# Fourier mixing and an MLP on one core: VectorE's sums of w2, a pinned opening, one load queue, filler matmuls

## The chip, the core and the metric

The kernel runs on one core of a Trainium2 chip. The core has TensorE (PE, matmuls and transposes, which write to PSUM), VectorE (DVE), ScalarE (ACT), GpSimd (POOL) and SyncE (SP, here only a queue that issues DMA transfers). Each engine works through its own queue in order and waits on semaphores for the others. The metric is the device time of one execution in microseconds; lower is better.

## The reference

Input x is 2048 x 576. Its rows are normalized (layernorm without weights) to xn, and the output is a sum of three terms:

```python
a = einsum("bsd,ed->bse", xn, dft_hid_re)
b = einsum("bsd,ed->bse", xn, dft_hid_im)
y = einsum("ts,bse->bte", dft_seq_re, a) - einsum("ts,bse->bte", dft_seq_im, b)
h = maximum(einsum("bsd,df->bsf", xn, w1), 0)
return x + y + einsum("bsf,fd->bsd", h, w2)
```

w1 is 576 x 4608 and w2 is 4608 x 576. All inputs are float32.

## The kernel before

**Numbers.** A float32 operand is scaled by a power of two and split into two float16 halves, hi on ScalarE (L164) and lo = src * s - hi on VectorE (L165). A product then takes three float16 products (hi hi, hi lo, lo hi). The power of two comes from a maximum of absolute values: for w1 by VectorE (`magnitude`, L98), for w2 as a sum of absolute values by ScalarE (`sum_w2`, L374). For blocks 0 and 1 the maximum over partitions goes through TensorE (`power_pe`, L134 to L157: a small matmul, a reduction on VectorE, a second small matmul, three small VectorE steps); for later blocks GpSimd does it.

**Tiling.** x is 16 tiles of 128 rows, four of them a group of 512. The hidden width is nine blocks of 512, each in four slices of 128. For each block and group the first layer (`mlp1`) is 4 x 14 matmuls of 512 columns; `mlp1_out` applies the ReLU, splits, and forms the sums of a Strassen-Winograd scheme; the second layer (`mlp2`) is seven products of 12 matmuls of 288 columns, each followed by an accumulation into `acc` in SBUF on VectorE (L334). Products 0, 2, 4 and 6 use one PSUM bank pair and add up in it, 1 uses another, 3 and 5 a third; so product 2 can start only after the accumulation of product 0 has read the bank. The scheme needs four sums of quarters of w2 for each half block (`sums_w2`, L404 to L407): they are made by GpSimd for blocks 0 and 1 and by VectorE for later blocks. The DFT follows after the nine blocks.

**The opening.** x is loaded into `acc`, tile by tile, and w1 into a pool of two buffers (tag `raw`) which w2 shares. Each tile of x is normalized: `stats` (L175: two statistics, a merge, a square root on ScalarE and six small steps on VectorE), `normalize` (L219: xn on VectorE, its float16 half from x on ScalarE), `remainder` (L227: xn minus its half, on GpSimd but for tile 0) and `transposes` (L236: nine transposes on TensorE into a PSUM slot, then two copies to SBUF on ScalarE, L245 and L248). In block 0 the first layer runs tile by tile for tiles 0 to 3, and for tiles 4 to 7 in the first two slices (`tile_by`, groups of 14 matmuls of 128 columns), so that it can start on the first tile. `power_pe`, `transposes`, the first layer's sums for tiles 4 to 7 (`pq`) and `mlp2` take their PSUM from one pool of two slots (tag `ps2`).

**What sets the order.** The code is written through a scheduler, which places the instructions of each engine in an order of its own choice, by program order as a priority and by its estimate of when operands are ready. Nothing of the opening is pinned. `weave` (L208) interleaves the small steps of the statistics with other calls. x and most of w1 are issued from SyncE's queue; w1's first half block from ScalarE's (L446). The main loop (L605) runs over pairs of block and group: at each step it issues the first layer of this pair, the second layer of the previous pair, and pieces of the next block's preparation from a list (`todo`, `prepare_block`).

Of the kernel before, what the change touches and what calls it, by code (L numbers as in the profile page):

```python
# [41 lines left out]
def kernel(  # L42
# [43 lines left out]
    def load_w1(b, i, parts=1, eng=nc.sync):  # L86
        r = raws["w1", b, i] = raw.tile([P, 2 * KT, P], F32, tag="raw", name=f"raw_w1_{b}_{i}")
        n = 2 * KT // parts
        for k in range(0, 2 * KT, n):
            eng.dma_start(r[:, k : k + n], w1[b, i][:, k : k + n])  # L90
# [5 lines left out]
    def magnitude(dst, src):  # L96

        nc.vector.tensor_reduce(dst, src, AX.XY, ALU.max, apply_absolute_value=True)  # L98

    def power(s, p, m):  # L100
# [12 lines left out]
        )  # L113

# [19 lines left out]
    def power_pe(s, p, m):  # L134
# [4 lines left out]
        for c in range(n):  # L139
            nc.tensor.matmul(  # L140
                ps[:1, 0, c * P : (c + 1) * P], m[:, c : c + 1], ident.bitcast(BF16),
                start=True, stop=True,
            )
        top = small.tile([1, n], BF16, tag=f"top{n}", name="top")
        nc.vector.tensor_reduce(
            top, ps[:1, 0, : n * P].rearrange("p (n f) -> p n f", f=P), AX.X, ALU.max
        )
        nc.tensor.matmul(ps[:, 1, :n], ones, top, start=True, stop=True)
        half = small.tile([P, n], F32, tag=f"half{n}", name="half")
        nc.vector.tensor_scalar(half, ps[:, 1, :n], 2.0**-107, 2.0**6, ALU.max, ALU.mult)  # L150
        nc.vector.tensor_scalar(
            s.bitcast(I32), half.bitcast(I32), EXPONENT, EXPONENT,
            ALU.bitwise_and, ALU.bitwise_xor,
        )
        nc.vector.tensor_scalar(
            p.bitcast(I32), half.bitcast(I32), EXPONENT, None, ALU.bitwise_and
        )  # L157
# [4 lines left out]
    def split(hi, lo, src, s):  # L162

        nc.scalar.activation(hi, src, AF.Copy, scale=s)  # L164
        nc.vector.scalar_tensor_tensor(lo, src, s, hi, ALU.mult, ALU.subtract)  # L165
# [9 lines left out]
    def stats(ts):  # L175
# [3 lines left out]
        sts = [small.tile([P, 2, 6], F32, tag="st", name=f"st{t}", bufs=4) for t in ts]  # L179
        for t, st in zip(ts, sts):  # L180
            for j in range(2):
                nc.vector.bn_stats(st[:, j, :], acc[t][:, j * EH : (j + 1) * EH])
                yield
        for i, st in enumerate(sts):
            nc.vector.bn_aggr(mv[:, i], st.rearrange("p a b -> p (a b)"))
            yield
# [13 lines left out]
        nc.vector.tensor_scalar(u, u, -0.5 * SX, 1.5 * SX, ALU.mult, ALU.add)  # L200
        yield
        nc.vector.tensor_tensor(r, u, r0, ALU.mult)
        yield
        stt(sh, m, -1.0, r, ALU.mult, ALU.mult)
# [3 lines left out]
    def weave(steps, *others):  # L208

        others = list(others)  # L210
        for _ in steps:
            if others:
                others.pop(0)()
        for f in others:
            f()

    xns, xss = {}, {}

    def normalize(t, eng=nc.vector):  # L219
# [4 lines left out]
        eng.tensor_scalar(xn, acc[t], means[t], factors[t], ALU.subtract, ALU.mult)  # L224
        nc.scalar.activation(xs[:, :D], acc[t], AF.Identity, bias=shifts[t], scale=factors[t])

    def remainder(t, eng):  # L227
        xn, xs = xns[t], xss[t]
        eng.tensor_tensor(
            xs[:, D : D + REM], xn[:, KM * P :], xs[:, KM * P : D], ALU.subtract  # L230
        )
        eng.tensor_tensor(
            xs[:, D + REM :], xn[:, : KM * P], xs[:, : KM * P], ALU.subtract
        )

    def transposes(t):  # L236
        xs = xss[t]
        pt = ps2.tile([P, 2, 1024], F16, tag="ps2", name=f"pt{t}")
        for k in range(NKX):
            nc.tensor.transpose(  # L240
                pt[:, k // 8, (k % 8) * P : (k % 8 + 1) * P], xs[:, k * P : (k + 1) * P], ident
            )
        g, c = divmod(t, TG)
        dst = xT[g][:, :, c * P : (c + 1) * P]
        nc.scalar.activation(  # L245
            dst[:, :8, :], pt[:, 0, :].rearrange("p (k t) -> p k t", t=P), AF.Copy
        )
        nc.scalar.activation(dst[:, 8, :], pt[:, 1, :P], AF.Copy)  # L248
# [35 lines left out]
    def mlp1_group(b, g, i, cols, ps, wk=WK):  # L284
        for n, (kx, hl, k) in enumerate(wk):
            nc.tensor.matmul(  # L286
                ps[:, cols], w1s[b, i // 2][:, hl, i % 2 * KT + k], xT[g][:, kx, cols],
                start=(n == 0), stop=(n == len(WK) - 1),
            )
# [6 lines left out]
    def mlp1_out(b, g, i, pa, pb):  # L296
# [6 lines left out]
        nc.scalar.activation(r21, a21, AF.Relu)  # L303
        for q, src in ((slice(A11, A11 + 1), a11), (slice(A12, A22 + 1), pb)):
            hi, lo = (h[:, n, q].rearrange("p a b -> p (a b)") for n in range(2))
            nc.scalar.activation(hi, src, AF.Relu)  # L306
            stt(lo, src, 0.0, hi, ALU.max, ALU.subtract)  # L307
        stt(s3, a11, 0.0, r21, ALU.max, ALU.subtract)
        stt(s1, a22, 0.0, r21, ALU.max, ALU.add)
        stt(s2, a22, 0.0, s3, ALU.max, ALU.subtract)  # L310
        stt(s4, a12, 0.0, s2, ALU.max, ALU.subtract)  # L311
        hi, lo = (h[:, n, S1 : S4 + 1] for n in range(2))
        order["s"] = nc.scalar.activation(hi, st[:, 1:], AF.Copy).ins  # L313
        nc.vector.tensor_tensor(lo, st[:, 1:], hi, ALU.subtract)  # L314
# [3 lines left out]
    def mlp2(b, g, n):  # L318
# [5 lines left out]
        for c in range(2):  # L324
            for i in range(NQ):
                h, w = hs[b, g, i], w2s[b, i]
                for j, (x, y) in enumerate(((0, 0), (0, 1), (1, 0))):
                    nc.tensor.matmul(  # L328
# [3 lines left out]
                    )  # L332
        o = accs[g].rearrange("p (h c) (j e) -> p h j c e", h=2, j=2)[:, row, col]
        nc.vector.scalar_tensor_tensor(o, ps, us[b], o, ALU.mult, ALU.add)  # L334
# [6 lines left out]
    def max_w1(b, f):  # L341
# [7 lines left out]
        magnitude(mx["f", b][:, r : r + 1], raws["w1", b, i][:, r * KT : (r + 1) * KT])  # L349
        if r:  # L350
            m = mx["w1", b][:, i : i + 1] if b > 1 else mx["b", i]
            nc.vector.tensor_reduce(m, mx["f", b], AX.X, ALU.max)

    def power_w1(b, i):
# [3 lines left out]
        else:  # L358
            power_pe(s, p, mx["b", i])
# [8 lines left out]
    def sum_w2(b, i):  # L368
# [5 lines left out]
        nc.scalar.activation(  # L374
            junk, raws["w2", b, i], AF.Abs, scale=2.0**-10, accum_out=mx["w2", b][:, i : i + 1]
        )

    def power_w2(b):
# [3 lines left out]
        else:  # L382
            m = small.tile([P, NQ], BF16, tag="mb2", name=f"mb2_{b}")
            nc.vector.tensor_copy(m, mx["w2", b])
# [452 lines left out]
```

## Time and profile before

| | us |
|---|---|
| median of 3 runs (lowest to highest) | 1305.89 (1304.32 to 1306.62) |
| profiled execution | 1306.57 |
| its span | 1304.8 |
| TensorE busy in the span | 1274.5 |
| VectorE busy | 968.0 |
| ScalarE busy | 532.8 |
| GpSimd busy | 49.7 |

Times of the trace count from the span's start. A group of instructions is shown by line, engine, operation, output and inputs with their shapes and count, then the total busy time and the mean of one in ns, then the idle time of its engine just before them with what ended it. In a table of stages each engine has its busy time and its count of instructions in that stretch, in the order PE, PE's weight loads, DVE, ACT, POOL; then come the granted TensorE clock as a share of full speed, the share of the DMA engines and GB/s. A row of waits names the engine and line that waited, what it waited for, the total, the number of times and the longest.

### The profile page before, as it was taken

What the parts mean: (1) busy time and instruction counts of PE and PEld (TensorE: products, weight loads), DVE (VectorE), ACT (ScalarE), POOL (GpSimd) and SP (SyncE); (2) the same over time, 40 slices, a digit from 0 to 9 for tenths busy, and PEclk for the clock granted to TensorE, in tenths of its full rate; (3) what the DMA queues carried; (4) which work ended last, traced back from release to release, by engine and by line L of the source; (5) the groups of instructions that cost most, each with busy time, mean ns of one, the idle gap of its engine ahead of it and who ended that gap; (6) DMA issues with size and microseconds to landing.
All of it is one profiled execution on the core that took longest, in us unless ns stands there. A gap on an engine that the chain in (4) does not pass through costs nothing.

```text
span 1304.8 us, 21675 instructions
## 1 busy us (share of the span) xinstructions
PE 1274.5 (98%) x9066; PEld 871.2 (67%) x9066; DVE 968.0 (74%) x1655; ACT 532.8 (41%) x794; POOL 49.7 (4%) x76
## 2 busy tenths in 40 slices
PE   7799999999999999999999999999999999999998
PEld 6565566666666666666666656677777777777777
DVE  8857778577596686785875885568678887878875
ACT  5634344344343443533433433234443333333332
POOL 2412000000000000000000000000000000000000
PEclk8899899999999999999999999999999999999999
DMA  6101213122122131131221222240014334243420
GB/s 238 42 1 55 76 49 116 58 73 87 48 89 85 49 107 68 49 125 49 74 93 41 94 94 85 91 149 17 1 52 172 131 128 159 98 146 121 142 84 19
DMA packets 38002, 112.75 MB, mean 86 GB/s; under 512 B 3984, under 2 KB 10640, under 8 KB 37904
## 3 DMA queue, kind: packets, MB, share of 16 engines
q1 hardware_dynamic: 37616, 110.71, 25.4%
q8 instruction: 71, 1.16, 0.4%
q10 hardware_dynamic: 288, 0.66, 0.1%
q14 instruction: 27, 0.22, 0.1%
HBM read 101.91 MB, written 9.44 MB: 85 GB/s over the span
## 4 chain that ended last, share of the span: by engine, by line
PE 89%; DVE 5%; ACT 2%; POOL 2%; DMA 1%; issue 1%; POOLq 0%; ACTq 0%; SPq 0%; DVEq 0%
PE p L286 30%; PE p L328 25%; PE p L771 25%; PE pd L670 8%; DVE acc L334 1%; DMA raw_d<-in_dft_dram 1%; ACT xT L245 0%; DVE h L314 0%; DVE w2s L165 0%; DVE h L307 0%; DMA raw_w<-in_w_dram 0%; POOL raw_w L407 0%; PE pt L240 0%; DVE c_md L98 0%; POOL raw_w L404 0%
## 5 line engine op out<-in xcount | busy, mean ns | idle before, releaser
L286 PE MATMUL p<-xT,w1s 128*128 128x512 f16 (+1 forms) x2268 | 466.3, 359 | 4.6 <-ACT xT L245 4.5
L328 PE MATMUL p<-w2s,h 128*128 128x288 f16 x3024 | 397.7, 288 | 14.3 <-ACT xT L248 7.8
L328 PEld LDWEIGHTS <-h 128*128 128x128 f16 x3024 | 296.8, 98 | 117.1 <-issue 15.3
L286 PEld LDWEIGHTS <-w1s 128*128 128x128 f16 x2268 | 210.0, 99 | 209.1 <-issue 9.1
L771 PE MATMUL p<-R,cs 128*128 128x288 f16 x2688 | 329.4, 287 | 0.0
L771 PEld LDWEIGHTS <-cs 128*128 128x128 f16 x2688 | 262.9, 98 | 66.3
L334 DVE SCALAR_TENSOR_TENSOR acc<-p,c_ub,acc 128x576 f32<-128x576 f32 x252 | 204.0, 812 | 19.3 <-PE p L328 18.9
L164 ACT ACTIVATE cs<-c,sc_c 128x1024 f16<-128x1024 f32 x112 | 128.5, 1148 | 202.0 <-PE p L771 147.6
L307 DVE SCALAR_TENSOR_TENSOR h<-p,h 128x256 f16<-128x256 f32 (+1 forms) x144 | 80.0, 555 | 148.6 <-ACT h L306 148.3
L165 DVE SCALAR_TENSOR_TENSOR cs<-c,sc_c,cs 128x1024 f16<-128x1024 f32 x112 | 143.7, 1283 | 50.2 <-ACT cs L164 42.9
L306 ACT ACTIVATE h<-p 128x256 f16<-128x256 f32 (+1 forms) x144 | 69.5, 485 | 236.9 <-PE p L286 236.9
L313 ACT ACTIVATE h<-s 128x1024 f16<-128x1024 f32 x72 | 76.1, 1058 | 166.6 <-DVE s L311 166.3
L670 PE MATMUL pd<-dsp,xT 128*128 128x288 f16 x896 | 109.9, 287 | 0.9 <-DVE acc L334 0.9
L314 DVE TENSOR_TENSOR h<-s,h 128x1024 f16<-128x1024 f32 x72 | 88.9, 1235 | 28.7 <-ACT h L313 28.6
L670 PEld LDWEIGHTS <-xT 128*128 128x128 f16 x896 | 87.6, 98 | 23.2 <-issue 1.1
L777 DVE SCALAR_TENSOR_TENSOR o<-p,us_c,o 128x288 f32<-128x288 f32 x112 | 57.5, 513 | 20.3 <-PE p L771 20.3
L598 ACT ACTIVATE f<-f 128x1024 f32<-128x1024 f32 x64 | 66.6, 1041 | 3.6 <-DMA f<-in_cre_dram 3.6
L165 DVE SCALAR_TENSOR_TENSOR w2s<-raw_w,c_sw,w2s 128x576 f16<-128x576 f32 (+1 forms) x54 | 48.2, 940 | 16.0 <-ACT w2s L164 16.0
L164 ACT ACTIVATE w2s<-raw_w,c_sw 128x576 f16<-128x576 f32 (+1 forms) x54 | 44.4, 850 | 36.7 <-DVE c_sw L396 19.0
L303 ACT ACTIVATE s<-p 128x256 f32<-128x256 f32 x72 | 26.7, 370 | 24.0 <-PE p L286 24.0
L688 ACT ACTIVATE R<-pd,c_rho 128x288 f16<-128x288 f32 x48 | 23.8, 499 | 22.2 <-DVE T L682 12.4
L165 DVE SCALAR_TENSOR_TENSOR w1s<-raw_w,c_sw,w1s 128x640 f16<-128x640 f32 x36 | 30.9, 878 | 0.1
(100 smaller groups left out, 623.8 us busy)
## 6 DMA issues: line engine op xcount, KB each, us to landing
f<-in_cre_dram SPq DMA_DIRECT2D x32, 512.0 KB, 3.5
f<-in_cim_dram SPq DMA_DIRECT2D x32, 512.0 KB, 3.5
c<-in_cre_dram SPq DMA_DIRECT2D x32, 512.0 KB, 3.9
c<-in_cim_dram SPq DMA_DIRECT2D x32, 512.0 KB, 4.5
raw_w<-in_w_dram SPq DMA_DIRECT2D x17, 640.0 KB, 4.0
raw_w<-in_w_dram SPq DMA_DIRECT2D x18, 576.0 KB, 4.0
acc<-in_x_dram SPq DMA_DIRECT2D x16, 288.0 KB, 6.1
spill<-acc SPq DMA_DIRECT2D x16, 288.0 KB, 2.5
```

Source lines behind the costliest of these rows:

```text
L164: nc.scalar.activation(hi, src, AF.Copy, scale=s)
L165: nc.vector.scalar_tensor_tensor(lo, src, s, hi, ALU.mult, ALU.subtract)
L286: nc.tensor.matmul(ps[:, cols], w1s[b, i // 2][:, hl, i % 2 * KT + k], xT[g][:, kx, cols], start=(n == 0), stop=(n == len(WK) - 1),)
L306: nc.scalar.activation(hi, src, AF.Relu)
L307: stt(lo, src, 0.0, hi, ALU.max, ALU.subtract)
L313: order["s"] = nc.scalar.activation(hi, st[:, 1:], AF.Copy).ins
L314: nc.vector.tensor_tensor(lo, st[:, 1:], hi, ALU.subtract)
L328: nc.tensor.matmul(ps[:, c], h[:, x, qa, c * P : (c + 1) * P], w[:, y, qb], start=first and i == 0 and j == 0, stop=i == NQ - 1 and j == 2 ...
L334: nc.vector.scalar_tensor_tensor(o, ps, us[b], o, ALU.mult, ALU.add)
L598: nc.scalar.activation(f, f, AF.Abs, scale=2.0**-10, accum_out=sums_c[:, n, q : q + 1])
L670: nc.tensor.matmul(ps[j], xT[g][:, kx, c * P : (c + 1) * P], dsp[j][:, hl, k], start=(n == 0), stop=(n == len(XK) - 1),)
L771: nc.tensor.matmul(ps, w[:, a, k], r[:, c, rq], start=first and k == 0 and j == 0, stop=k == HK - 1 and j == 2, skip_group_check=not first,)
```

## The change

Five things change; all lie in the preparation of blocks 0 and 1 and in the steps ahead of the main loop.

1. `sums_w2` is done by VectorE in all blocks.
2. `pin` ties an instruction behind the one traced before it on its engine, an order of issue with no wait. Every instruction of the opening goes through it until `pinned.clear()`, so each engine runs the opening in the order of the program text.
3. The opening is rewritten in a new order, and reaches further: it now holds step (block 0, group 1) with the second layer of group 0 and the statistics and transposes of tiles 8 to 11, and the main loop starts one step later. The statistics merge tile by tile. For all tiles but 0 to 3 the float16 half is made from xn (`early=False`), not from x. Tile 0's transposes and copies are cut in parts.
4. x tile 0, both halves of w1's first half block, tiles 1 and 2, and w1's second half block are issued from SyncE's queue in this order; w1's first had been issued from ScalarE's queue.
5. Filler matmuls on zeros: 34 ahead of the first tile (32 before) and 14 more inside the scale computation of w1's first half.

In the main loop the statistics of tiles 12 to 15, and the magnitudes of w1 of block 1, are placed behind the last first-layer output's final VectorE instruction (`issue_after(order["lo"])`).

```diff
-    load_w1(0, 0, 2, nc.scalar)
-    warm = const.tile([P, 1], F32, name="warm")
-    nc.scalar.activation(warm, eps, AF.Sqrt)
     load_x(0)
+    load_w1(0, 0, 2)
     load_x(1)
+    load_x(2)
     load_w1(0, 1)
-    for t in range(2, 2 * TG):
+    for t in range(3, 2 * TG):
         load_x(t)
...
+    pinned = [True]
+
+    def pin(ins):
+        return tc.keep_in_program_order(ins) if pinned else ins
...
     def sums_w2(b, i):
-        tt = (nc.vector if b > 1 else nc.gpsimd).tensor_tensor
-        tt(b11, b12, b11, ALU.subtract)
+        tt = nc.vector.tensor_tensor
+        pin(tt(b11, b12, b11, ALU.subtract))
...
-        magnitude(mx["f", b][:, r : r + 1], raws["w1", b, i][:, r * KT : (r + 1) * KT])
+        with tc.issue_after(order["lo"]) if b == 1 else nullcontext():
+            magnitude(mx["f", b][:, r : r + 1], raws["w1", b, i][:, r * KT : (r + 1) * KT])
...
     def mlp2(b, g, n, between=()):
...
+        for f in between:
+            f()
         o = accs[g].rearrange("p (h c) (j e) -> p h j c e", h=2, j=2)[:, row, col]
-        nc.vector.scalar_tensor_tensor(o, ps, us[b], o, ALU.mult, ALU.add)
+        pin(nc.vector.scalar_tensor_tensor(o, ps, us[b], o, ALU.mult, ALU.add))
...
+    def normalize(t, early=False):
+        pin(nc.vector.tensor_scalar(xn, acc[t], means[t], factors[t], ALU.subtract, ALU.mult))
+        if early:
+            pin(nc.scalar.activation(
+                xs[:, :D], acc[t], AF.Identity, bias=shifts[t], scale=factors[t]
+            ))
+        else:
+            pin(nc.scalar.activation(xs[:, :D], xn, AF.Copy))
```

The new opening (`N`, `E`, `T` are normalize, remainder and transposes; `run` runs a generator to its end, `next` to its next `yield`, which `stats` has after each tile's merge and after the square root, and `power_pe` after each of its two matmul steps):

```python
    def fill(n):
        for _ in range(n):
            pin(nc.tensor.matmul(ps[3][:, :256], idle[:, :P], idle, start=True, stop=True))
    fill(34)
    s0, s1, s23, s4 = (stats(ts) for ts in ([0], [1], [2, 3], [4, 5, 6, 7]))
    next(s0)
    next(s0)
    max_w1(0, 0)
    run(s0)
    N(0, early=True)
    T(0, range(4), ())
    max_w1(0, 1)
    E(0, V, (0,))
    w = power_w1(0, 0)
    next(w)
    T(0, range(4, 5), ((0, 5),))
    next(s1)
    next(w)
    fill(14)
    run(w)
    E(0, V, (1,))
    next(s1)
    T(0, range(5, 9), ())
    split_w1(0, 0)
    T(0, (), ((5, 9),))
    tile_by(0, (0,), ps, WK0)
    run(s1)
    N(1, early=True)
    split_w1(0, 1)
    tile_by(0, (1,), ps, WK0)
    E(1, GP)
    T(1)
    next(s23)
    max_w1(0, 2)
    tile_by(1, (0, 1), ps)
    next(s23)
    next(s23)
    max_w1(0, 3)
    run(s23)
    w = power_w1(0, 1)
    next(w)
    N(2, early=True)
    N(3, early=True)
    next(w)
    E(2, GP)
    E(3, GP)
    run(w)
    T(2)
    split_w1(0, 2)
    tile_by(2, (0, 1), ps)
    split_w1(0, 3)
    T(3)
    tile_by(0, (2,), ps)
    tile_by(3, (0, 1), ps)
    tile_by(1, (2,), ps)
    for _ in range(4):
        next(s4)
    tile_by(0, (3,), ps)
    tile_by(1, (3,), ps)
    next(s4)
    run(s4)
    for t in range(TG, 2 * TG):
        N(t)
        E(t, GP)
    tile_by(2, (2, 3), ps)
    tile_by(3, (2, 3), ps)
    pq = ps2.tile([P, 2, 512], F32, tag="ps2", name="p1_0_1")
    qs = [pq[:, 0], pq[:, 1]]
    T(4)
    mlp1_out(0, 0, 0, *ps[:2])
    tile_by(4, (0, 1), qs)
    T(5)
    w = prepare_w2(0)
    w[0]()
    w[1]()
    tile_by(5, (0, 1), qs)
    mlp1_out(0, 0, 1, *ps[2:])
    T(6)
    p = power_w2(0)
    next(p)
    tile_by(6, (0, 1), qs)
    next(p)
    T(7)
    run(p)
    w[3]()
    tile_by(7, (0, 1), qs)
    q2 = [mlp1(0, 1, 2), mlp1(0, 1, 3)]
    w[4]()
    mlp1_out(0, 1, 0, *qs)
    for f in w[5:]:
        f()
    s8 = stats(range(2 * TG, 3 * TG))
    st = lambda: next(s8)
    ne = lambda t: lambda: (N(t), E(t, GP))
    mlp2(0, 0, 0, (st, st))
    mlp2(0, 0, 1, (st, st, st))
    mlp2(0, 0, 2, (lambda: run(s8), ne(8)))
    mlp2(0, 0, 3, (ne(9),))
    mlp2(0, 0, 4, (ne(10), ne(11)))
    mlp2(0, 0, 5)
    T(8)
    mlp2(0, 0, 6)
    T(9)
    T(10)
    T(11)
    mlp1_out(0, 1, 1, *q2)
    pinned.clear()
```

In `prepare_w2`, steps 0 and 1 are `sum_w2`, step 2 the power, steps 3 and 4 the first split of w2 with `sums_w2` for its two halves, and the rest the four other splits.

More of the change, by code (lines that the diff above doesn't have):

```diff
@@ L1 @@
-from contextlib import ExitStack
+from contextlib import ExitStack, nullcontext
 import concourse.bass as bass
@@ L457 @@
         load_x(t)
+    warm = const.tile([P, 1], F32, name="warm")
+    nc.scalar.activation(warm, eps, AF.Sqrt)
     V, GP = nc.vector, nc.gpsimd
@@ L465, in tile_by @@
             mlp1_group(0, g, i, slice(c * P, (c + 1) * P), ps[i], wk)
-    no = lambda: None
+    def fill(n):
+        for _ in range(n):
+            pin(nc.tensor.matmul(ps[3][:, :256], idle[:, :P], idle, start=True, stop=True))
     N, E, T = normalize, remainder, transposes
-    for _ in range(32):
-        nc.tensor.matmul(ps[3][:, :256], idle[:, :P], idle, start=True, stop=True)
-    weave(stats([0]), no, no, no, lambda: max_w1(0, 0))
-    N(0)
-    max_w1(0, 1)
-    E(0, V)
-    power_w1(0, 0)
@@ L603 @@
     passes.append(lambda: sum_c(4 * len(units) - 1))
-    for n in range(1, len(steps)):
+    for n in range(2, len(steps)):
         b, g = steps[n]
@@ L617 @@
                 todo += [scales_d]
-        if b == 0 and g + 1 < NG:
-            weave(stats([(g + 1) * TG + i for i in range(TG)]))
+        if n == 2:
+            with tc.issue_after(order["lo"]):
+                run(stats(range(3 * TG, NT)))
         ps = []
         for i in range(NF):
-            if n > 1 or i > 1:
-                ps.append(mlp1(b, g, i))
-                if i % 2:
-                    mlp1_out(b, g, i // 2, *ps[-2:])
-            if b == 0 and g + 1 < NG:
-                t = (g + 1) * TG + i
+            ps.append(mlp1(b, g, i))
+            if i % 2:
+                mlp1_out(b, g, i // 2, *ps[-2:])
+            if n == 2:
+                t = 3 * TG + i
                 normalize(t)
```

208 lines of the change are left out of this document (92 added, 116 removed).

## The prediction

> **What bounds the kernel now.** I read the page first, for the span and the engines' shares, then a table of stages, the waits of the first 160 us, the timeline around each gap of TensorE, and last the groups of instructions by form for durations.
>
> ```profile
> span 1304.8 us, 21675 instructions
> ```
>
> The profiled execution took 1306.57 us, so 1.8 us lie around its span; the median of the runs is 1305.89, 0.7 below it. The stages (TensorE's busy time first, the granted clock after the engines):
>
> ```profile
> 13.20:16.40 3.20, 3.17 (x31) 3.17 (x31) 2.99 (x12) 1.31 (x3) 1.01 (x2) 0.50 0.66 208
> 16.40:44.00 27.60, 23.29 (x385) 21.67 (x384) 25.71 (x92) 23.16 (x40) 13.37 (x19) 1.00 0.30 104
> 50.00:56.90 6.90, 0.04 (x2) 0.02 (x1) 5.17 (x9) 3.25 (x7) 5.55 (x6) 0.79 0.25 77
> 56.90:60.60 3.70, 3.70 (x16) 2.35 (x16) 2.11 (x2) 2.36 (x5) 1.42 (x2) 0.50 0.60 201
> 74.30:77.60 3.30, 3.30 (x9) 1.25 (x9) 1.16 (x3) 3.10 (x5) 2.39 (x4) 0.52 0.02 5
> 77.60:128.00 50.40, 50.12 (x330) 29.92 (x329) 31.50 (x62) 21.68 (x35) 10.35 (x12) 1.00 0.08 24
> 128.00:133.40 5.40, 1.67 (x13) 1.20 (x13) 3.91 (x8) 1.26 (x2) 1.58 (x2) 0.91 0.56 174
> 133.40:139.40 6.00, 6.00 (x20) 2.87 (x20) 6.00 (x12) 1.60 (x3) 0.38 (x1) 0.51 0.15 61
> 160.00:300.00 140.00, 140.00 (x879) 85.72 (x877) 103.78 (x201) 58.38 (x99) 2.14 (x6) 1.00 0.23 75
> ```
>
> From 160 us on TensorE is full at clock 1.00: nothing there is touched. The losses that the change can reach are the opening up to 77 us and the hole at 128 to 139. The second hole costs 5.4 - 1.67 = 3.7 us idle and half of 6.0 at clock 0.51 = 3.0, together 6.7. The first costs 6.9 idle and 1.85 at half clock. What makes the holes:
>
> ```profile
> ACT w2s L164 <- POOL raw_w L405: 6.7, 4, 2.8
> ACT w2s L164 <- POOL raw_w L407: 6.3, 4, 1.9
> PE p L328 <- ACT xT L248: 7.8, 2, 6.9
> PE p L328 <- DVE acc L334: 3.9, 2, 3.4
> ```
>
> ```profile
> 4.58 0.82 DVE L182 BATCH_NORM_STATS2 st<-acc 128x6 f32<-128x288 f32 x2 [1.32 <-DMA acc<-in_x_dram]
> 25.34 3.29 PE L286 MATMUL p<-xT,w1s 128*128 128x128 f16 x56
> 55.89 0.78 ACT L164 ACTIVATE w2s<-raw_w,c_sw 128x576 f16<-128x576 f32 x1 [1.75 <-POOL raw_w L407]
> 56.58 0.26 ACT L248 ACTIVATE xT<-pt 128x128 f16<-128x128 f16 x1
> 74.26 1.29 PE L286 MATMUL p<-xT,w1s 128*128 128x512 f16 x3 [1.11 <-ACT xT L245]
> ```
>
> GpSimd makes the sums of w2, ScalarE's splits wait for them (13 us), and in the first hole one small copy out of the transposes' PSUM (56.58) stands behind those splits in ScalarE's queue and holds the slot that the first second-layer product needs. In the second it is an accumulation on VectorE behind a split. The row at 74.26 is my mark: there the first layer of group 2 of block 0 starts, with group 0's second layer complete. Where that mark falls in the changed kernel decides the sign.
>
> **The change, part by part.** Durations for all parts:
>
> ```profile
> L334 DVE SCALAR_TENSOR_TENSOR acc<-p,c_ub,acc 128x576 f32<-128x576 f32 x41 | 33.3, 812 | 4.3 <-PE p L328 4.2
> L314 DVE TENSOR_TENSOR h<-s,h 128x1024 f16<-128x1024 f32 x13 | 16.8, 1291 | 5.1 <-ACT h L313 5.0
> L245 ACT ACTIVATE xT<-pt 128x1024 f16<-128x1024 f16 x16 | 16.5, 1032 | 13.2 <-PE pt L240 13.0
> L313 ACT ACTIVATE h<-s 128x1024 f16<-128x1024 f32 x13 | 13.8, 1060 | 15.8 <-DVE s L311 15.6
> L182 DVE BATCH_NORM_STATS2 st<-acc 128x6 f32<-128x288 f32 x32 | 13.0, 442 | 1.3 <-DMA acc<-in_x_dram 1.3
> L165 DVE SCALAR_TENSOR_TENSOR w2s<-raw_w,c_sw,w2s 128x576 f16<-128x576 f32 x12 | 10.9, 927 | 8.2 <-ACT w2s L164 8.2
> L307 DVE SCALAR_TENSOR_TENSOR h<-p,h 128x512 f16<-128x512 f32 x14 | 9.6, 689 | 12.6 <-ACT h L306 12.4
> L98 DVE TENSOR_REDUCE c_mf<-raw_w 128x1 f32<-128x640 f32 x12 | 9.5, 804 | 0.3 <-DMA raw_w<-in_w_dram 0.3
> L224 DVE TENSOR_SCALAR xn<-acc,mv,r 128x576 f32<-128x576 f32 x16 | 8.6, 578 | 0.0
> L306 ACT ACTIVATE h<-p 128x512 f16<-128x512 f32 x14 | 8.4, 601 | 30.8 <-PE p L286 30.8
> L374 ACT ACTIVATE j<-raw_w 128x1152 f32<-128x1152 f32 x6 | 7.0, 1173 | 2.3 <-DMA raw_w<-in_w_dram 2.3
> L165 DVE SCALAR_TENSOR_TENSOR w2s<-raw_w,c_sw,w2s 128x864 f16<-128x864 f32 x6 | 6.4, 1112 | 1.4 <-ACT w2s L164 1.4
> L308 DVE SCALAR_TENSOR_TENSOR s<-p,s 128x256 f32<-128x256 f32 x14 | 5.8, 416 | 0.0
> L164 ACT ACTIVATE w2s<-raw_w,c_sw 128x864 f16<-128x864 f32 x6 | 5.8, 1005 | 4.2 <-DVE c_sw L396 4.2
> L248 ACT ACTIVATE xT<-pt 128x128 f16<-128x128 f16 x16 | 4.6, 285 | 0.0
> L404 DVE TENSOR_TENSOR raw_w<-raw_w 128x288 f32<-128x288 f32 x2 | 0.8, 448 | 0.0
> L200 DVE TENSOR_SCALAR u<-u 128x4 f32<-128x4 f32 x3 | 0.5, 160 | 0.0
> ```
>
> Consecutive instructions of one engine overlap by about 0.08 us. A matmul's own cost is read off the chain of waits:
>
> ```profile
> 85.68 0.50 PE pt L240 x9
> 89.12 3.02 PE p L286 x14
> 92.14 2.94 PE p L328 x24
> ```
>
> *The sums.* Eight subtractions a block at 0.448 = 3.6 us of VectorE for each of blocks 0 and 1. In block 1 VectorE is busy 31.5 of 50.4 us before the hole, so they fit, and the hole's 6.7 us go. In block 0 they enter a stretch where VectorE is the limit (below).
>
> *One queue.* x tile 0 is no longer shared with w1. Its statistics start at 4.58 now; the bounds are no gain and 1.3 us (the whole wait); I take 1.0, so 3.6. It saves only what the next steps hand on.
>
> *Pins, start to tile 3.* VectorE's written order up to the scale of w1's second half is: 8 statistics at 0.44 with 4 merges at 0.2 (4.3), 4 reductions at 0.80 and 2 merges (3.5), three chains of six dependent small steps at 0.16 and a handoff (3.4), 4 normalizations (2.3), tile 0's remainder (0.9), two scales (1.3), two splits (1.8): 17.5. Less some 1 us of overlap, plus 1.5 in which it stands behind ScalarE's splits, it ends at 3.6 + 18 = 21.6. Tile 2's remainder (GpSimd) and transposes give its copies at 22.8 to 24.0; the two high halves of w1's splits stand behind these on ScalarE (25.5), then tile 3's copies end at 27.6. TensorE has by then 7 of its 16 groups of 14; the other 9, 126 matmuls at 3.29/56, take 7.4: 35.05. A good clock after the fillers would save up to the 1.6 us of 13.2 to 16.4, but not here: the limit is VectorE.
>
> *Pins, tiles 4 to 7.* ScalarE's queue now reads: copies of T4, first-layer output (0,0,0), copies of T5, the two magnitude passes over w2, output (0,0,1), copies of T6, T7. An output is one round trip: two 256-wide copies and a 512-wide one on ScalarE, 0.69 + 4 x 0.416 less overlaps on VectorE, then 1.06 back on ScalarE: 4.3 us, and whatever is queued behind it waits. T4: transposes 0.5, 0.2 to ScalarE, copies 1.2: 36.95. Output: 41.3. Copies T5: 42.5. Magnitudes, with their accumulator reads 2 x 1.35: 45.1. Output: 49.4. Copies T6: 50.5. TensorE's pieces in between are 1.65 each, so it idles 3.3 and then 6 us. VectorE's last piece of the output ends at 50.65, then the scale of w2: 0.5 to the first small matmul, tile 6's 28 matmuls at half clock after that hole (3.1): 54.1; scale, T7 (it needs the slot that the scale's read frees) and copies: 56.4; the first split of w2 on ScalarE 1.0: 57.4.
>
> *Pins, to the mark.* From here VectorE runs in one written line: two splits at 1.1 and eight sums (2.2 + 3.5), output (0,1,0) with its wait for ScalarE (2.5 + 1.1 + 1.2), four splits at 0.73: 70.7. TensorE's tile 7 and 28 first-layer matmuls (1.65 + 6.04) end at 64.2 and two second-layer products (2.94) at 67.2, but the third adds into the bank of the first, which is read only after those splits and two tiles' statistics (1.9): 73.4. From there products of 1.47 (2.9 at half clock, since TensorE idled 6 us) alternate with VectorE's five further accumulations (3.75), two more tiles' statistics (1.9), the chain of small steps (1.1) and four normalizations (2.1): with 0.4 of waiting the sixth accumulation ends at 82.7. It frees the bank of T8; T8 to T11, two at a time with 1.2 of copies each, end at 88.9.
>
> So the mark moves from 74.3 to 88.9: +14.6. The removed 6.9 and 1.85 are inside that number.
>
> *After the mark.* VectorE has left over what it has now done before the mark: statistics and normalizations of tiles 12 to 15 (8 x 0.44 + 1.1 + 2.3 = 7) and four reductions of block 1 (3.2). In the 50.4 us ahead of block 1 it then holds 31.5 + 10.2 + 3.6 = 45.3 us. I charge 1 us for local waits; 0 and 5 are the bounds. The half clock at 74.3 (1.65) I keep, for this row:
>
> ```profile
> 70.90:74.30 3.40, 1.37 (x21) 1.12 (x19) 3.40 (x11) 2.30 (x5) 0.00 (x0) 1.00 0.00 0
> ```
>
> TensorE was busy in 1.37 of those 3.4 us, with no gap over 1.1, and was at half clock after it; my T9 to T11 leave it some 1.5 of 3.4.
>
> [...]
>
> Sum: 14.6 - 6.7 + 1 = +8.9 on 1306.57, or 1315.5; less 0.7 to stand beside the median, and rounded down for the clock that may hold: **1314 us**.
>
> **The rivals.** *Sums free, pins free* (faster): the in-order queues cost nothing that the present order doesn't cost. Then 6.9 + 1.85, 1.65 and 6.7 go, 17 us, less up to 3.6 for VectorE's sums: about 1290. For it: 13 us of waits on GpSimd are in the trace. Against: it needs T5's and T6's copies not to stand behind the outputs, and the written order puts them there. It decides at the mark: before 74.3 + 6.7 = 81 the kernel is faster. *Pins bind less than written*: the order stays near today's and only the sums move: the same 17 us less half of those 3.6, and 1291. *Even*: my walk is 6 to 8 us too slow (say, output round trips overlap with the copies): mark near 81, 1306. *Dearer*: VectorE, 45 of 50 us loaded, holds TensorE through groups 2 and 3, for the bound of 5 us in place of 1 and two more half-clock windows (2 x 1.65): 1321.
>
> **How the numbers follow.** Chances: my forecast (1309 to 1319) 0.52; dearer 0.12; even 0.12; free pins 0.19; pins that do not bind 0.05. A measurement of this kernel tells about 0.2% (2.6 us) from no change. So slower 0.64, the same 0.12, faster 0.24. The range must reach past the even case into the faster one and up to the dearer: 1296 to 1322; the forecast's own is 1309 to 1319.
>
> **What would show it.** Right: no matmul of the second layer waits on GpSimd, the hole at 128 is gone or only shifted, TensorE has gaps of 3 and 6 us ended by T5's and T6's copies on ScalarE, VectorE is full for 20 us before the mark, and the mark is at 85 to 92. Wrong: a mark before 81, copies that start while an output's round trip is open, or a wait of second-layer products in block 1 on VectorE's sums as long as that on GpSimd now.

## The result and the profile after

The changed kernel takes 1322.8 us (median of 4, 1321.6 to 1324.43), the kernel before 1305.11 beside it (4 runs, 1303.5 to 1306.62): a ratio of 1.0137 (95% interval 1.0119 to 1.0154), 17.7 us slower. The profiled execution of the changed kernel took 1322.82 us. First its page, then the table of stages (TensorE's busy time, its weight loads, VectorE, ScalarE, GpSimd, then the granted clock), cut at the places where the changed kernel changes pace:

```profile
span 1321.0 us, 21681 instructions
```

```profile
37.00:57.20 20.20, 9.54 (x115) 8.61 (x114) 9.16 (x24) 10.89 (x20) 2.48 (x3) 0.75 0.00 1
57.20:75.40 18.20, 10.88 (x81) 6.48 (x80) 14.97 (x29) 6.80 (x11) 0.00 (x0) 0.91 0.15 45
75.40:90.20 14.80, 11.84 (x96) 8.75 (x97) 9.42 (x22) 7.35 (x14) 6.28 (x8) 0.88 0.09 36
90.20:103.00 12.80, 12.25 (x56) 5.38 (x55) 11.09 (x35) 5.72 (x13) 0.00 (x0) 1.00 0.00 1
103.00:107.00 4.00, 2.24 (x17) 1.40 (x18) 4.00 (x5) 2.34 (x5) 3.20 (x4) 0.89 0.00 0
107.00:120.00 13.00, 11.92 (x95) 8.93 (x93) 9.86 (x17) 3.60 (x8) 3.48 (x5) 0.90 0.01 1
120.00:127.00 7.00, 5.38 (x26) 2.44 (x25) 5.06 (x13) 5.19 (x8) 0.00 (x0) 0.76 0.05 8
...
143.00:150.00 7.00, 6.72 (x39) 3.60 (x37) 7.00 (x15) 3.36 (x5) 0.00 (x0) 1.00 0.22 67
...
160.00:300.00 140.00, 140.00 (x879) 85.71 (x877) 102.94 (x198) 59.11 (x101) 2.18 (x6) 1.00 0.22 70
```

TensorE's timeline gives the mark (first layer of group 2), the first second-layer products and the first gaps behind the mark; then its longest waits of the first 170 us:

```profile
64.81 1.63 PE L331 MATMUL p<-w2s,h 128*128 128x288 f16 x12
67.55 1.64 PE L331 MATMUL p<-w2s,h 128*128 128x288 f16 x12 [1.10 <-DVE s L314]
75.40 7.97 PE L331 MATMUL p<-w2s,h 128*128 128x288 f16 x48 [6.21 <-DVE acc L339]
...
90.21 12.25 PE L289 MATMUL p<-xT,w1s 128*128 128x512 f16 x56 [1.34 <-ACT xT L249]
103.78 0.75 PE L245 MATMUL pt<-ident,xn 128*128 128x128 f16 x5 [1.32 <-ACT xn L228]
...
105.63 0.40 PE L245 MATMUL pt<-ident,xn 128*128 128x128 f16 x4 [0.86 <-POOL xn L235]
```

```profile
PE p L289 <- ACT xT L249: 9.9, 8, 3.2
PE p L331 <- DVE acc L339: 6.5, 2, 6.2
PE pm L146 <- DVE mb L390: 5.0, 1, 5.0
```

Two numbers divide the loss. The mark went from 74.26 to 90.21, 15.95 later. The rest of the span behind it is 1304.8 - 74.26 = 1230.54 before and 1321.0 - 90.21 = 1230.79 after: nothing gained, nothing lost. Yet the second hole is gone (143 to 150, block 1, is busy for 6.72 of 7.0). What it gave back was lost again just behind the mark: 0.55 + 1.76 + 1.08 + 1.62 us idle between 90 and 127 by the rows above, and two stretches at half clock. "Mark" and "rest" (span less mark, both of the profiled execution) are the two columns by which all kernels below are read. Each is from one execution, and a stretch at half clock, which loses some 1.7 us, followed two gaps in the kernel before and did not follow nearly the same two in e1 (last section); smaller differences in these columns are not read. One of the four runs of e8 below, the profiled one, was disturbed (4410.88 us against 1324.86 to 1325.71), so e8 has no mark and no rest.

### The profile page after: what moved, and what is told of

Same layout as the page of the kernel before. It is cut to its first block, busy times and chain, and to the rows that moved or that the text cites. A ratio compares the mean times of both kernels' runs of the same rounds, so it can differ in the third digit from the quotient of the medians.

```text
span 1321.0 us, 21681 instructions
## 1 busy us (share of the span) xinstructions
PE 1279.6 (97%) x9082; PEld 876.8 (66%) x9082; DVE 977.5 (74%) x1671; ACT 531.8 (40%) x794; POOL 33.3 (3%) x60
## 4 chain that ended last, share of the span: by engine, by line
PE 87%; DVE 7%; issue 2%; ACT 2%; DMA 1%; POOL 0%; POOLq 0%; ACTq 0%
PE p L289 29%; PE p L827 25%; PE p L331 24%; PE pd L726 8%; DVE acc L339 1%; DMA raw_d<-in_dft_dram 1%; DVE w2s L173 1%; DVE h L317 1%; ACT xT L249 1%; DVE h L310 1%; PE pt L245 0%; POOL xn L235 0%; DVE c_md L98 0%; DVE st L190 0%; ACT h L316 0%
## 5 line engine op out<-in xcount | busy, mean ns | idle before, releaser
L331 PE MATMUL p<-w2s,h 128*128 128x288 f16 x3024 | 398.1, 288 | 11.4 <-DVE acc L339 8.5
L289 PEld LDWEIGHTS <-w1s 128*128 128x128 f16 x2268 | 213.6, 100 | 217.4 <-issue 13.6
L317 DVE TENSOR_TENSOR h<-s,h 128x1024 f16<-128x1024 f32 x72 | 87.9, 1221 | 31.0 <-ACT h L316 30.9
L833 DVE SCALAR_TENSOR_TENSOR o<-p,us_c,o 128x288 f32<-128x288 f32 x112 | 57.4, 512 | 20.8 <-PE p L827 20.7
L744 ACT ACTIVATE R<-pd,c_rho 128x288 f16<-128x288 f32 x48 | 23.9, 500 | 21.8 <-DVE T L738 12.0
```

The lines of the kernel that those rows point to most:

```text
L289: pin(nc.tensor.matmul(ps[:, cols], w1s[b, i // 2][:, hl, i % 2 * KT + k], xT[g][:, kx, cols], start=(n == 0), stop=(n == len(WK) - 1),))
L317: order["lo"] = pin(nc.vector.tensor_tensor(lo, st[:, 1:], hi, ALU.subtract)).ins
L331: pin(nc.tensor.matmul(ps[:, c], h[:, x, qa, c * P : (c + 1) * P], w[:, y, qb], start=first and i == 0 and j == 0, stop=i == NQ - 1 and j ...
```

## The experiments

Theories at the start: P, the pinned in-order queues cost the time; S, the sums are too much for VectorE; R, the rewritten text does it without pins. Once P stood, for the stretch before the mark: A, copies queued behind outputs on ScalarE; V, VectorE's written line; W, w2's magnitudes, scale and first split, which begins 13 us later than before. A+W is both at once. And T: behind the mark, the statistics of tiles 12 to 15 come too late. Each ratio below is against runs of the kernel before on the same chip.

| kernel | median us | ratio to before (95% interval) | mark | rest |
|---|---|---|---|---|
| before | 1305.11 | | 74.26 | 1230.5 |
| changed | 1322.80 | 1.0137 (1.0119 to 1.0154) | 90.21 | 1230.8 |
| e1 sums only | 1297.25 | 0.9926 (0.9910 to 0.9942) | 73.66 | 1222.9 |
| e6 queue only | 1308.92 | 1.0018 (1.0009 to 1.0027) | 77.06 | 1230.5 |
| e7 sums and queue | 1297.49 | 0.9933 (0.9918 to 0.9948) | 73.30 | 1222.8 |
| e2 no pins | 1303.46 | 0.9976 (0.9966 to 0.9985) | 77.35 | 1224.1 |
| e3 pins to tile 3 | 1305.66 | 1.0004 (0.9994 to 1.0014) | 78.33 | 1224.1 |
| e4 pins, GpSimd sums | 1323.91 | 1.0139 (1.0122 to 1.0155) | 87.11 | 1233.7 |
| e8 copies first | 1325.66 | 1.0163 (1.0146 to 1.0180) | | |
| e9 statistics of 8 to 11 early | 1323.52 | 1.0149 (1.0128 to 1.0171) | 90.25 | 1230.8 |
| e10 and of 12 to 15 | 1319.70 | 1.0121 (1.0106 to 1.0137) | 92.54 | 1227.0 |
| e5 statistics untied | 1318.54 | 1.0108 (1.0093 to 1.0123) | 93.01 | 1222.4 |
| e11 w2 early | 1316.18 | 1.0078 (1.0063 to 1.0093) | 84.46 | 1230.5 |
| e12 w2 early, untied | 1313.77 | 1.0056 (1.0039 to 1.0073) | 88.20 | 1224.0 |
| e13 w2 and copies early | 1320.23 | 1.0107 (1.0090 to 1.0124) | 88.01 | 1233.0 |
| e14 all of it | 1311.20 | 1.0042 (1.0027 to 1.0057) | 86.06 | 1222.6 |

### The parts by themselves

**e1**, the kernel before with the sums on VectorE:

```diff
-        tt = (nc.vector if b > 1 else nc.gpsimd).tensor_tensor
+        tt = nc.vector.tensor_tensor
```

> Only the sums of w2 of blocks 0 and 1 go to VectorE, all else as before. Theory P (the pinned in-order queues cost the time, the sums themselves save it): the holes at 50 to 57 and 128 to 139 go, 13 us less up to 3.6 of VectorE's time, so about 1294 (1288 to 1300). Rival S (VectorE is too full for the sums in the opening): no gain, 1303 to 1310.

**e6**, the kernel before with the new order of loads (and ScalarE's warm-up square root behind them):

```diff
-    load_w1(0, 0, 2, nc.scalar)
     load_x(0)
+    load_w1(0, 0, 2)
     load_x(1)
+    load_x(2)
     load_w1(0, 1)
```

> The kernel before with the change's load order from SyncE's queue alone. Tile 0's statistics start 0.9 us earlier; by the walk little of it reaches the end: 1303 to 1306. If the start sets the whole opening: 1304 less 1, and if the scheduler orders badly on it, 1307 or more.

**e7**, both edits:

```diff
+        tt = nc.vector.tensor_tensor
...
+    load_w1(0, 0, 2)
```

> The kernel before with the sums on VectorE, and x and w1 issued from one queue in the changed order; no pins, no filler matmuls. If the queue's loss of about 3 us (1308.9 against 1305.9) adds to the sums' gain: 1299 to 1302. If the sums take it away, since VectorE no longer lets GpSimd's work set the first steps: 1296 to 1298.5.

Measured: the sums alone take 0.7% off, e7 is no slower than e1 and e6 alone is slightly slower than before. e1's gain is nearly all in the rest, 1230.5 to 1222.9: the hole at 128 goes. The first hole stays nearly whole. TensorE's timeline in e1:

```profile
48.06 1.63 PE L328 MATMUL p<-w2s,h 128*128 128x288 f16 x12 [0.52 <-ACT xT L248]
49.53 3.40 PE L286 MATMUL p<-xT,w1s 128*128 128x512 f16 x15
56.93 5.88 PE L328 MATMUL p<-w2s,h 128*128 128x288 f16 x24 [4.00 <-DVE s L311]
```

The first product starts at 48.06 in place of 56.88, but the second waits 4.00 us for VectorE, and half clock follows (a mean clock of 0.83 from 48 to 60 us and of 0.89 from 60 to 72): the wait on GpSimd is replaced by one on the engine that took its work. The rival "sums free, pins free" of the prediction had counted on both holes. In e6 the earlier x does reach TensorE, but the gain isn't handed on:

```profile
12.07 3.15 PE L286 MATMUL p<-xT,w1s 128*128 128x128 f16 x28 [1.11 <-ACT xT L245]
...
58.28 5.75 PE L328 MATMUL p<-w2s,h 128*128 128x288 f16 x24 [7.40 <-ACT xT L248]
```

The first tile starts 1.2 us earlier than before (13.23), the wait of the first hole grows from 6.86 to 7.40. With the sums on VectorE that wait is gone, and so is the queue's cost (e7).

### The pins

**e2**, the changed kernel without pins, and **e3**, with the pins dropped from tile 2's second slices on:

```diff
-    pinned = [True]
+    pinned = []
```

```diff
+    pinned.clear()
     tile_by(2, (2, 3), ps)
```

> The changed kernel with all pins off: same text, same queue, same fillers and sums, the scheduler chooses the order. Theory P: most of the loss goes, 1295 to 1305. Rival R (the rewritten text and its reach cost the time, not the pins): 1317 to 1324. Rival S: the same as R.

> The changed kernel with pins only up to the third and fourth slices of tiles 0 and 1; tiles 4 to 11, the outputs, the second layer of group 0 and the preparation of w2 are free. Theory P by the walk (tiles 0 to 3 cost 1 us, the rest 14): 1303 to 1310. If the pins of tiles 0 to 3 cost most, 1315 to 1323.

Without pins the changed kernel is 0.2% faster than before: P stands. The pins up to there are worth about 2 us (e3 against e2), those after it 17: 1322.8 against 1305.66 (the profiled spans are 18.6 apart, 11.9 in the mark and 6.7 in the rest). A smaller part belongs to R: e2 has e7's sums and queue and is 6.0 us slower, mostly at the mark (77.35 against 73.30); which of the text's new steps or fillers does it was not separated.

**e4**, the changed kernel with GpSimd's sums for blocks 0 and 1 again:

```diff
-        tt = nc.vector.tensor_tensor
+        tt = (nc.vector if b > 1 else nc.gpsimd).tensor_tensor
```

> The changed kernel with the sums of w2 of blocks 0 and 1 back on GpSimd, everything else as changed. Theory P (the order costs, the sums on VectorE pay also inside it): the products wait for GpSimd again before the mark and at 140 to 150, 1326 to 1335. Rival S (the sums overload VectorE's written line): VectorE's line loses 8 times 1.26 us before the mark, the mark falls to 82 to 86 and the time to 1312 to 1319.

Neither forecast fits: the time is that of the changed kernel. The mark is 3.1 earlier, since VectorE has less to do before it. The rest is 2.9 longer: ScalarE's splits of block 1 wait 6.7 us for GpSimd again, and between 127 and 153 TensorE waits 1.70 us for w2's scale, 1.03 for an output and 1.28 for an accumulation, where the longest such wait of the changed kernel is 0.28. Inside the pinned order the sums are even; outside they gain 8.7 us.

### Before the mark: VectorE's idle time

**e8**, the order of the text changed within the pins:

```diff
     T(4)
+    T(5)
+    tile_by(4, (0, 1), qs)
+    T(6)
+    tile_by(5, (0, 1), qs)
+    T(7)
     mlp1_out(0, 0, 0, *ps[:2])
-    tile_by(4, (0, 1), qs)
-    T(5)
```

(with tile 6's and 7's matmuls behind the outputs).

> The changed kernel, pinned, with T5 to T7 and their first-layer matmuls ahead of the two outputs, so that no transposes' copies stand behind an output on ScalarE. Theory V (VectorE's written line from 57 us on sets the mark, the start of group 2): the gaps of TensorE at 40 and 46 go, the mark stays within 3 us of 90.2, total 1319 to 1324. Theory A (copies behind outputs set the mark): mark at 82 to 85, total 1314 to 1318.

**e9**, the statistics and normalizations of tiles 8 to 11 taken from between the products to VectorE's idle stretches:

```diff
+    s8 = stats(range(2 * TG, 3 * TG))
+    for _ in range(4):
+        next(s8)
     T(4)
     mlp1_out(0, 0, 0, *ps[:2])
+    next(s8)
+    run(s8)
...
+    for t in (8, 9, 10):
+        N(t)
+        E(t, GP)
     T(7)
     run(p)
+    N(11)
+    E(11, GP)
```

**e10**, besides, the statistics of tiles 12 to 15:

```diff
+    s12 = stats(range(3 * TG, NT))
+    for _ in range(4):
+        next(s12)
...
-                run(stats(range(3 * TG, NT)))
+                run(s12)
```

> The changed kernel, pinned, with the statistics and normalizations of tiles 8 to 11 moved up into times in which VectorE stood idle (36 to 38, 43 to 46, 52 to 58), so that nothing stands between the second-layer products and their accumulations. Theory V: 7 us less in VectorE's line, mark at 82 to 85, total 1314 to 1318. Theory A: no change, 1321 to 1324.

> As the run before, and also the statistics of tiles 12 to 15 in the opening's idle time. Theory T (after the mark, tiles 12 to 15 come late and cost what the sums saved, about 9 us of gaps and half clock): a further 4 to 8 us less than the run with the statistics of 8 to 11 alone, 1307 to 1312. Rival (VectorE is simply full after the mark): 1 us or less.

No gain from e8, none at the mark from e9 or e10: A alone falls, and so does V in the form "the statistics in the line". For T, e10 is 3.8 us faster than e9, with a rest 3.8 shorter: a little under the 4 to 8 that T had named, and well over its rival's 1. In e9 TensorE's third product starts at 75.96, no earlier than 75.40: w2's first split has slipped to 59.30 on ScalarE, behind tile 11's half.

**e11**, w2's preparation moved up within the pins; tile 5's copies also go ahead of the output (0,0,0) and tile 6's ahead of (0,0,1):

```diff
+    w = prepare_w2(0)
+    w[0]()
     next(s4)
...
+    w[1]()
     tile_by(2, (2, 3), ps)
...
     T(4)
+    p = power_w2(0)
+    next(p)
+    next(p)
-    mlp1_out(0, 0, 0, *ps[:2])
     tile_by(4, (0, 1), qs)
+    run(p)
     T(5)
+    mlp1_out(0, 0, 0, *ps[:2])
+    w[3]()
     tile_by(5, (0, 1), qs)
-    mlp1_out(0, 0, 1, *ps[2:])
     T(6)
+    mlp1_out(0, 0, 1, *ps[2:])
```

(where the moved steps of w2 stood before, they are taken out; not shown).

**e13**, e11 with the copies further ahead (tile 6's before the output (0,0,0), tile 7's before (0,0,1)):

```diff
     T(5)
-    mlp1_out(0, 0, 0, *ps[:2])
-    w[3]()
     tile_by(5, (0, 1), qs)
     T(6)
-    mlp1_out(0, 0, 1, *ps[2:])
+    mlp1_out(0, 0, 0, *ps[:2])
+    w[3]()
     tile_by(6, (0, 1), qs)
     T(7)
     tile_by(7, (0, 1), qs)
+    mlp1_out(0, 0, 1, *ps[2:])
```

> The changed kernel with w2's preparation of block 0 moved up in the written order: its two sums of magnitudes on ScalarE before and after the normalizations of tiles 4 to 7, its scale before the matmuls of tile 4, its first split and sums before the matmuls of tile 5; tiles 5 and 6 are copied ahead of the outputs (0,0,0) and (0,0,1). Theory W (the line from w2's magnitudes over scale, split and sums to the products sets the mark, and the pins put it 13 us late): the first split of w2 begins at 44 to 48 instead of 57.2, the mark falls from 90.2 to 78 to 84, and 8 to 12 of the 1322.8 us go, to 1311 to 1315. Rival V (VectorE's whole load up to the mark sets it, in whatever order): the mark stays within 2 us of 90.2 and the time at 1321 to 1325.

> The kernel with w2's preparation moved up, and the copies and matmuls of tiles 5 to 7 placed ahead as well: tile 5's and tile 6's copies before the output (0,0,0), tile 7's before the output (0,0,1). Theory A+W (the first product waits for two lines, TensorE's tiles behind ScalarE's outputs and w2's preparation; lifting one alone shows little, as the copies alone and w2 alone did): TensorE's waits of 4.1 and 3.1 us for the copies of tiles 6 and 7 shrink, the first product falls from 63.7 to 59 to 61, the mark from 84.5 to 80 to 82, and the time from 1316.2 to 1311 to 1314. Rival V (VectorE's line sets the third product whatever the first does): the third product stays within 1 us of 69.7, the mark within 1 us of 84.5, the time at 1315 to 1317.

e11's first split came at 45.69, 11.5 us earlier, but the mark only 5.75 earlier and the time 6.6 us less, where W had named 6 to 12 and 8 to 12: W holds in part, and since e11 moved two copies too, not all of that need be w2's. e13 fell on V's side, and further: TensorE's first product came earlier (61.88 against 63.73), the third product later (72.75 against 69.66), the time 4 us worse. What sets the third product is seen when VectorE is counted from 37 us up to its first accumulation, which frees the third product's bank. First that accumulation, in VectorE's timeline of the changed kernel and of e3:

```profile
74.57 0.77 DVE L339 SCALAR_TENSOR_TENSOR acc<-p,c_ub,acc 128x576 f32<-128x576 f32 x1
```

```profile
62.78 0.81 DVE L339 SCALAR_TENSOR_TENSOR acc<-p,c_ub,acc 128x576 f32<-128x576 f32 x1
```

Then one row each of the stage table, up to it (the third number in the row of engines is VectorE's): the changed kernel, e3, e11, e13.

```profile
37.00:74.60 37.60, 20.42 (x195) 15.08 (x193) 23.33 (x52) 17.70 (x30) 2.48 (x3) 0.83 0.06 19
```

```profile
37.00:62.80 25.80, 17.24 (x190) 12.48 (x188) 23.86 (x58) 16.92 (x30) 11.63 (x14) 1.00 0.09 26
```

```profile
37.00:68.80 31.80, 20.82 (x194) 15.64 (x192) 23.86 (x50) 15.44 (x26) 2.25 (x3) 0.89 0.07 21
```

```profile
37.00:71.90 34.90, 21.11 (x203) 15.01 (x200) 23.49 (x50) 15.51 (x26) 2.30 (x3) 0.89 0.06 20
```

VectorE has nearly the same amount of work in all four, 23.3 to 23.9 us. Its idle time differs: 14.3 us in the changed kernel, 1.9 where the scheduler orders the engine, 7.9 in e11, 11.4 in e13. And from the first accumulation to the mark it is 15.5 to 16.1 us in each. So among these four the mark moves with VectorE's idle time in the written order: the engine stands through each output's round trip to ScalarE and through w2's scale, with other work queued behind the waiting instruction (in the changed kernel 11.3 us of waits on ScalarE's steps of the outputs, the longest 4.5, and 3.3 on the scale's two small matmuls). e3 has the first output behind it by then, and fills the waits with the statistics and normalizations of tiles 8 to 11. e13 let VectorE wait 5.71 us for the later first output, and lost what e11 had won. Idle time that is filled with later work alone gains nothing, though: in e9 VectorE works 27.2 us and is idle for 10.9 up to its first accumulation, which still starts at 75.09, because w2's scale and split come no earlier.

### Behind the mark: the tie and the pinned output

**e5**, the changed kernel with the statistics of tiles 12 to 15 free:

```diff
-            with tc.issue_after(order["lo"]):
-                run(stats(range(3 * TG, NT)))
+            run(stats(range(3 * TG, NT)))
```

**e12** is e11 with this edit. **e14** is e13 with the same statistics free, and with the statistics of tiles 8 to 11 where VectorE waited for the first output:

```diff
+    s8 = stats(range(2 * TG, 3 * TG))
...
+    next(s8)
+    next(s8)
     T(5)
     tile_by(5, (0, 1), qs)
+    next(s8)
+    next(s8)
```

> The changed kernel with one edit: the statistics of tiles 12 to 15 no longer tied behind the last output's final instruction on VectorE. Theory T: the scheduler takes them into earlier idle time, TensorE's gaps between 102 and 124 shrink, total 1314 to 1319. If the tie costs nothing: 1321 to 1324; if they now delay the accumulations before the mark: 1324 or more.

> The kernel with w2's preparation moved up, and besides the statistics of tiles 12 to 15 no longer tied behind the output (0,1,1). Theories W and T together (the late mark costs 8 to 12, the tie 4 to 5 after it, and the two add): 1306 to 1311. If the tie matters only because the mark is late, as a rival has it, the second edit is worth under 2 us on top of the first: 1310 to 1315 where the first alone gives 1311 to 1315. If V holds: 1318 to 1320, as the freed statistics alone.

> The same, with the statistics of tiles 8 to 11 also placed early (four merges around tile 5's transposes, between two outputs) and those of tiles 12 to 15 not tied behind the output (0,1,1). With A+W and T: the third product no longer waits for two tiles' statistics (1.9 us), mark at 78 to 81, the gaps after the mark go: 1305 to 1309. If VectorE's load itself is the limit (rival V), the statistics only move the delay: 1311 to 1315.

The edit lets the mark slip by 2.8 us (e5) and 3.7 (e12), since the scheduler now puts statistics between the products, and shortens the rest by 8.4 and 6.5. Net, by the medians, it gains 4.3 and 2.4 us. T stands in e5; in e12 the gain lies between T's 4 to 5 and the rival's "under 2". e14's 1311.2 is 2 us above what A+W and T together had named, in V's range: its VectorE line is 5.0 us idle up to the first accumulation at 70.6, with 28.62 us of work in it.

How the tie costs is seen on VectorE and GpSimd in the changed kernel (L317 is the last step of an output, L190 statistics, L222 normalization, L235 remainders):

```profile
95.13 1.23 DVE L317 TENSOR_TENSOR h<-s,h 128x1024 f16<-128x1024 f32 x1 [0.19 <-ACT h L316]
96.27 1.17 DVE L190 BATCH_NORM_STATS2 st<-acc 128x6 f32<-128x288 f32 x3
...
102.37 0.57 DVE L222 TENSOR_SCALAR xn<-acc,mv,r 128x576 f32<-128x576 f32 x1
...
103.80 3.37 POOL L235 TENSOR_TENSOR xn<-xn 128x64 f16<-128x64 f32 x4 [17.24 <-ACT xn L228]
```

and on VectorE in e2, where the tie is kept and the pins are gone:

```profile
71.80 1.23 DVE L317 TENSOR_TENSOR h<-s,h 128x1024 f16<-128x1024 f32 x1 [0.40 <-ACT h L316]
73.67 1.17 DVE L190 BATCH_NORM_STATS2 st<-acc 128x6 f32<-128x288 f32 x3
...
78.75 2.05 DVE L222 TENSOR_SCALAR xn<-acc,mv,r 128x576 f32<-128x576 f32 x4
```

Without the pins the tie shows no cost (no run took it out there): in e2 the output (0,1,1) ends at 73, ahead of the mark at 77.35, the statistics follow it, and TensorE's timeline shows no wait from the mark to 119 us. The pins put that output behind tile 11's copies, so it ends at 96.4, 6 us after the mark; the statistics, the chain of small steps, the normalization and the remainders follow one another, and TensorE's queue stands at tile 12's transposes at 103.78 with second-layer products behind them. In e5 TensorE has no gap there:

```profile
93.00:107.00 14.00, 13.99 (x93) 8.68 (x93) 9.82 (x18) 8.20 (x16) 5.17 (x6) 1.00 0.00 0
107.00:120.00 13.00, 12.93 (x89) 7.60 (x88) 9.28 (x20) 6.02 (x10) 0.00 (x0) 1.00 0.00 1
120.00:127.00 7.00, 7.00 (x45) 3.98 (x43) 5.22 (x12) 3.18 (x6) 0.00 (x0) 1.00 0.26 84
```

e1, the one-line change, beats both kernels; the fastest with the rewritten opening, e2, stays 6 us above it. What sets e14's remaining distance from e3 beyond VectorE's line was not taken further.

## Why the prediction was right and wrong

The direction and the main cause were right: the pinned order was the reason, and the mark decided. The walk to the mark holds step by step:

| step | forecast | measured |
|---|---|---|
| tile 0's statistics start | 3.6 | 3.7 |
| tile 3's copies end | 27.6 | 29.4 |
| tile 5's copies end | 42.5 | 43.6 |
| tile 6's copies end | 50.5 | 51.3 |
| first split of w2 ends | 57.4 | 58.2 |
| VectorE's splits end | 70.7 | 72.8 |
| third product starts | 73.4 | 75.4 |
| mark | 88.9 | 90.2 |

It is 1.8 us short at tile 3's copies, 2.1 at VectorE's splits and 1.3 at the mark. The signs that it named are there: no second-layer product waits on GpSimd, TensorE has a gap of 3.2 us that tile 5's copies end and one of 5.0 that w2's scale ends where I had tile 6's copies, and VectorE's line is full from 58 us to the third product but for an output's round trip.

**The step that failed** is the one behind the mark: "I charge 1 us for local waits; 0 and 5 are the bounds." With 6.7 us of the second hole taken off, the rest was to be 1230.5 - 5.7 = 1224.8. It is 1230.8. The sums did take that hole, so the term that I put at 1 us, with 5 as its upper bound, came to 7.0. The rows from 90 to 127 hold it: 5.0 us idle and two stretches at half clock of 1.7 each, less the 1.65 that I had kept at the mark and that did not come, make 6.75. e5 shows what opens the gaps: with only the tie cut they are gone, and both half-clock stretches with them. The rest is 8.4 us shorter there; 2.8 of that come back as a later mark. I had seen the work ("statistics and normalizations of tiles 12 to 15") and weighed it only as VectorE's load, 45.3 of 50.4 us; over the 50.4 us behind the mark VectorE was busy for 38.3. It is a matter of order: the work is tied behind an output that is pinned behind the mark, and it is then a serial chain in front of TensorE. VectorE is full only while that chain runs (10.1 of 10.2 us from 96.4 to 106.6); from 107 to 127 it is not, by the rows 9.86 of 13.0 us and 5.06 of 7.0, and TensorE still has gaps.

The rival "dearer" had the size (1321) and "two more half-clock windows", both of which came; its mechanism, VectorE's load through groups 2 and 3, is not what e5 shows, since there VectorE does the same work, with a mark 2.8 us later, and the gaps are gone.

**The clock at the mark.** I kept 1.65 us there, by the row of the kernel before at 70.90. It did not come: TensorE was busy for 2.26 of the 3.41 us from 89.06, and from 90.2 to 103 the clock is 1.00. The 0.8 us that I rounded down "for the clock that may hold" are shown by no run; the changed kernel held its clock there and saved the whole 1.65. Behind the next gaps, none above 1.32 us, it ran at 0.50 (from 106.13 and from 123.19). The last section shows nearly the same two gaps ahead of the mark with the clock halved behind them in the kernel before and held in e1, which the prediction could not know.

**The queue.** I took 1.0 us of gain at the start, and "only what the next steps hand on". e6 shows that they hand on nothing: the first tile starts earlier and the first hole is longer.

**The sums in block 0.** I had them enter "a stretch where VectorE is the limit". e4 shows 3.1 us at the mark for 3.6 us of subtractions: right.

## What to carry to other kernels

What the written order cost here is what its engines wait, not what they work: count, for each engine, the idle time that stands behind each pinned wait, and ask whether what it waits for can come earlier. Other work put into the wait gained nothing at the mark by itself (e9). Where a tie ("issue this after that") exists, see where the order puts what it hangs on: a tie that shows no cost behind an early instruction became a serial chain behind a late one. Try each part of a change alone; here one line of it gave 0.7% and the other parts took 2%.

## What the runs showed of the hardware

Behind its mark the changed kernel's clock halved twice, each time after short gaps, none above 1.32 us. In steps of 0.1 us, the granted clock drops at 106.1 and 123.2 and is back at 109.6 and 126.6. In the first 160 us of its trace and of that of the kernel before there are nine stretches at half clock: 13.65, 10.24, 6.83, 3.41 and 3.41 us long in the one, 6.83, 6.83, 3.41 and 6.83 in the other. All are multiples of 3.41, and so are the stretches at full clock between them (17.07, 17.07, 27.31 and 13.65; 37.55, 13.65 and 54.61). The stage tables of the changed kernel, the kernel before and e1, cut in such steps:

```profile
89.06:92.47 3.41, 2.26 (x11) 1.07 (x11) 1.49 (x4) 2.31 (x7) 0.00 (x0) 1.00 0.00 0
102.72:106.13 3.41, 1.37 (x14) 0.85 (x15) 3.41 (x5) 1.75 (x4) 2.33 (x4) 1.00 0.00 0
106.13:109.54 3.41, 3.41 (x17) 2.18 (x15) 2.52 (x5) 1.70 (x3) 2.46 (x3) 0.50 0.00 0
119.78:123.19 3.41, 1.79 (x19) 1.05 (x17) 1.95 (x8) 2.25 (x4) 0.00 (x0) 1.00 0.00 0
123.19:126.60 3.41, 3.41 (x9) 1.26 (x9) 2.71 (x6) 3.00 (x5) 0.00 (x0) 0.50 0.00 0
```

```profile
71.05:74.46 3.41, 1.38 (x19) 1.03 (x18) 3.41 (x10) 2.46 (x5) 0.00 (x0) 1.00 0.00 0
74.46:77.87 3.41, 3.41 (x9) 1.22 (x8) 1.00 (x3) 2.94 (x4) 2.66 (x4) 0.50 0.02 5
```

```profile
69.45:72.86 3.41, 2.19 (x27) 1.72 (x25) 3.41 (x9) 1.47 (x3) 0.00 (x0) 1.00 0.00 0
72.86:76.27 3.41, 2.61 (x13) 1.19 (x13) 2.71 (x7) 3.41 (x6) 1.67 (x2) 1.00 0.02 5
76.27:79.68 3.41, 3.41 (x32) 2.62 (x31) 1.57 (x3) 2.27 (x5) 3.41 (x7) 1.00 0.00 0
```

Twice, TensorE of the changed kernel was busy for only part of a step, 1.37 and 1.79 of 3.41 us, with no gap above 1.32, and ran the next 3.41 us at half clock, which loses 1.7 us. The kernel before and e1 have nearly the same two gaps ahead of the mark (0.92 and 1.11 us, 0.91 and 1.11). In the kernel before both fall into one step and the clock halves; in e1 most of the second falls into the next row and it does not. e4 has the changed kernel's four gaps behind its mark (1.32, 0.86, 1.04 and 0.91 us; 1.32, 0.86, 1.03 and 0.91 in the changed kernel) and keeps a clock of 1.00 through them, from 100 to 127 us. In the traces of the kernel before and of the changed kernel, 71 steps at full clock start between 10 and 160 us: each of the 8 with half clock behind them held 1.80 us of TensorE work or less, and each of the 63 others 2.05 or more. The work of e3 from 73.65 to 77.06 is 27 transposes and nothing else of TensorE, 1.83 us, and its clock is 1.00 from 72 to 84 us. No run set the busy share on purpose, so 1.80 and 2.05 are what the steps of these two traces held and not a law.
